# One ring of eleven buffers for loads and stores, dV and dK stored in separate halves, and dense row products on the tensor engine alone

## The chip, the cores and the metric

The kernel runs on one core of one Trainium2 chip. The metric is the device time of one execution in microseconds (us). The measured times of one kernel within one set of runs differ by up to about 1.5%, so each kernel was timed in five rounds against the kernel before on the same chip, apart from the first comparison of before and after (four runs each).

## The reference

The reference is a forward pass and its gradient: attention over a cache, a feed-forward part, the same attention again with the same weights and cache, and the same feed-forward part again. There is one query token, so every product with a weight matrix is a matrix times a vector.

```
B, Sq, D = 1, 1, 1024;  Hq, Hkv, Sk, Dh = 32, 4, 65536, 128;  F = 3584      # all bf16
x = x + attn(layernorm(x), k_cache, v_cache, wq, wo)      # called layer L1
x = x + ffn(layernorm(x), w1, b1, w2, b2)                 # L2
x = x + attn(layernorm(x), k_cache, v_cache, wq, wo)      # L3
x = x + ffn(layernorm(x), w1, b1, w2, b2)                 # L4
_out, _vjp = jax.vjp(_f, x, k_cache, v_cache, wq, wo, w1, b1, w2, b2)
return (_out, *_vjp(grad_out))                            # gradients of the caches too
```

K and V together are 128 MB. The kernel reads them four times. Sweeps 1 and 2 are the forward attentions of L1 and L3. Sweep 3 is the backward pass of L3 that finds only dq. Sweep 4 is the backward pass of L1 and makes dK and dV for both layers at once. It also stores 128 MB of dK and dV and, in the background, some 31 MB of weight gradients. Between the sweeps lie dense stages (called gap 1, gap 2, gap 3 below), which need weights but no cache.

## The kernel before

Loads of the cache come in blocks of 1 MB, 8 KB in each of 128 partitions. Six buffers of a kept pool hold blocks from one sweep to the next, which walks the other way, and six more stream. In sweep 4 the streaming six make room for staging tiles of 2 MB, two of them:

```
stpool = stack.enter_context(tc.tile_pool(name="b4_st", bufs=2))
...
def k8(g, c8):                       # eight columns of K and V at a time
    ...
    if j0 == 0:
        state["st"] = stpool.tile([P, 2, J, DH], BF, name="gst", tag="gst")   # J = 32, DH = 128
    stg = state["st"]
    ...
    for half in range(2):
        pg = ps_gg()                 # [P, 1024] f32, 2 buffers
        for t2 in range(2):          # t2 = 0 is dK, 1 is dV
            nc.tensor.matmul(pg[:, 512 * t2:512 * t2 + 512], lhsT=xt[64 * t2:64 * t2 + 64, j0 // 4 + half, :],
                             rhs=GG[64 * t2:64 * t2 + 64, :, :].rearrange("p a b -> p (a b)"), ...)
        jj = j0 + 4 * half
        evac(stg[:, :, jj:jj + 4, :]..., pg[:, :]..., kind="f32")   # ACT or DVE, whichever has less to do
    if j0 + 8 == J:                  # the block is whole: two stores of 1 MB
        nc.gpsimd.dma_start(out=GKv[g][b], in_=stg[:, 0, :, :])
        nc.gpsimd.dma_start(out=GVv[g][b], in_=stg[:, 1, :, :])
```

The softmax weights were kept as one tile for each layer, `eT[P, G, R, C]`, in which the columns c of one head are neighbours. Sweep 4 took them in two products on DVE and copied them on POOL:

```
nc.vector.tensor_tensor(out=X[:, :, 0:R],  in0=ps_dp[:, :, 0:R],  in1=ea, op=ALU.mult)
nc.vector.tensor_tensor(out=X[:, :, R:R2], in0=ps_dp[:, :, R:R2], in1=eb, op=ALU.mult)
nc.gpsimd.tensor_copy(out=X[:, :, R2:3 * R], in_=ea)
nc.gpsimd.tensor_copy(out=X[:, :, 3 * R:R4], in_=eb)
```

A dense product along the rows of a weight matrix (for which this kernel has PE transpose the weights first) was given, 128 x 1024 weights at a time, to whichever engine a running estimate called least busy: DVE multiplies and sums (A), DVE multiplies and ACT sums (B), or PE transposes and multiplies after a copy by DVE (C) or ACT (D).

```
best = min(opts, key=lambda k: (max(opts[k]), sum(opts[k])))
if best == "A":   nc.vector.scalar_tensor_tensor(..., accum_out=yout)
elif best == "B": nc.vector.tensor_tensor(...); nc.scalar.activation(..., accum_out=yout)
else:             # C, D: 8 transposes, a copy out of PSUM, 8 matmuls of one column
```

## Time and profile before

The kernel before takes 2182.95 us (median of 4 runs, 2175.93 to 2195.28). Its profiled execution has a span of 2178.0 us. I cut the span at the first matmul of each sweep with a transposed block of the cache and at the last one into its output or dq, and some 20 us lie before sweep 1. The first view is the page of the profile. Its rows of digits are 40 equal slices of the span: the clock that was granted to TensorE in tenths, the DMA engines' busy share in tenths, and what they moved.

```profile
PE 1713.9 (79%) x29802; PEld 1353.1 (62%) x29802; DVE 1238.8 (57%) x2298; ACT 1081.2 (50%) x1672; POOL 219.6 (10%) x416
...
PEclk9999998599999966999999667888888878887888
DMA  9999999889999997999999839899998999999996
GB/s 383 418 416 416 418 416 402 310 345 415 419 415 417 417 377 264 406 414 418 416 416 419 315 112 359 318 346 369 386 356 357 347 364 364 379 354 349 396 353 249
```

A row of slices at 414 to 419 GB/s is a sweep in which the transfers leave no hole: a faster engine can shorten it only at its ends. The three dips (310, 264, 112 GB/s) are the three dense stages, where the clock falls to 5 or 6 tenths. After the third, in sweep 4, no slice but one is above 390. The windows view gives the same by stretch. Its columns are the length, each engine's busy time and instruction count, the clock, the DMA share and GB/s.

```profile
395.00:432.00 37.00, 12.68 (x268) 11.42 (x267) 35.40 (x68) 5.07 (x8) 0.00 (x0) 0.50 0.77 277
800.00:850.00 50.00, 18.82 (x238) 15.71 (x238) 34.11 (x81) 26.81 (x46) 0.00 (x0) 0.53 0.78 288
1211.00:1290.00 79.00, 50.83 (x655) 43.85 (x655) 56.02 (x157) 45.69 (x69) 1.19 (x2) 0.56 0.58 210
1440.00:2060.00 620.00, 517.11 (x5982) 313.99 (x5982) 417.42 (x571) 389.38 (x417) 156.44 (x279) 0.84 0.94 366
```

In the first dense stage DVE is busy 35.4 of 37 us. In the third no engine is full: DVE, PE and ACT wait for one another. In sweep 4 (the last line) the DMA share is 0.94. The view of the staging tile says what its writers waited for, as time in us and number of waits.

```profile
its engine sat idle before it (us, times) until:
  PE ps_gg L829: 201.0, 203
  DMA out_dram<-gst: 154.4, 44
```

Waiting for PE is waiting for work. Waiting 154 us for an earlier store to land is a lack of buffers. Last, the groups of instructions that the change touches, with busy time, mean ns of one, and the idle time before them.

```profile
L143 ACT CAST gst<-ps_gg 128x1024 bf16<-128x1024 f32 x296 | 296.5, 1016 | 210.2 <-PE ps_gg L829 114.0 <-DMA out_dram<-gst 89.9 <-ACT gst L143 1.2
L146 DVE CAST gst<-ps_gg 128x1024 bf16<-128x1024 f32 x216 | 262.9, 1220 | 160.4 <-PE ps_gg L829 86.9 <-DMA out_dram<-gst 64.4 <-issue 3.1
...
L580 ACT ACTIVATE L_eT<-S_sb,L_negm 128x128 bf16<-128x128 f32 x256 | 99.1, 390 | 27.5 <-DVE L_negm L576 27.5
...
L796 DVE TENSOR_TENSOR X<-ps_sc,L_eT 128x256 bf16<-128x256 f32 x64 | 36.9, 577 | 0.0
...
L690 DVE TENSOR_TENSOR dsT<-ps_sc,L_eT 128x512 bf16<-128x512 f32 x32 | 32.6, 1019 | 31.8 <-PE ps_sc L685 31.8
```

### The profile page before, as it was taken

Reading aid. Unit: us, or ns where it says so; the run is one execution under the profiler, and the core shown is the slowest. Engines: PE = TensorE matmul, PEld = TensorE weight load, DVE = VectorE, ACT = ScalarE, POOL = GpSimd, SP = SyncE. Lnnn points to the kernel's source line nnn. Section 1 sums busy time; section 2 is a strip of 40 time slices with the busy share of each in tenths; the row PEclk is TensorE's granted clock in tenths of the full one; section 3 lists DMA queues with packets and bytes.
Section 4 is the critical chain, followed back from the end, with each engine's and each line's share of the span. In section 5 each row is a group of like instructions: output and inputs, shape, how many; then the busy total and the mean of one; then the engine's idle time right before and its main releaser. Section 6 shows DMA issues by size and latency. Waiting matters only on the chain. (4 is left out here: it accounts for less than half of the span.)

```text
span 2178.0 us, 66787 instructions
## 1 busy us (share of the span) xinstructions
PE 1713.9 (79%) x29802; PEld 1353.1 (62%) x29802; DVE 1238.8 (57%) x2298; ACT 1081.2 (50%) x1672; POOL 219.6 (10%) x416
## 2 busy tenths in 40 slices
PE   7888887488888855878787767788879888888877
PEld 6877776388777744777777655445545545445444
DVE  3545443645445437644444668666757666666766
ACT  3434443044444416543433556566656556665655
POOL 0000000000000000000000001222222222222222
PEclk9999998599999966999999667888888878887888
DMA  9999999889999997999999839899998999999996
GB/s 383 418 416 416 418 416 402 310 345 415 419 415 417 417 377 264 406 414 418 416 416 419 315 112 359 318 346 369 386 356 357 347 364 364 379 354 349 396 353 249
DMA packets 149226, 806.51 MB, mean 370 GB/s; under 512 B 14012, under 2 KB 14026, under 8 KB 69322
## 3 DMA queue, kind: packets, MB, share of 16 engines
q1 hardware_dynamic: 120714, 636.54, 74.1%
q0 software_dynamic: 28224, 165.70, 18.6%
q8 instruction: 233, 3.82, 0.7%
q14 instruction: 55, 0.45, 0.1%
HBM read 636.50 MB, written 165.69 MB: 368 GB/s over the span
## 5 line engine op out<-in xcount | busy, mean ns | idle before, releaser
L146 DVE COPY kt<-ps_tr 128x1024 bf16<-128x1024 bf16 x667 | 449.4, 686 | 366.9 <-PE ps_tr L524 191.7
L143 ACT COPY kt<-ps_tr 128x1024 bf16<-128x1024 bf16 x357 | 357.4, 1014 | 494.8 <-PE ps_tr L524 301.0
L143 ACT CAST gst<-ps_gg 128x1024 bf16<-128x1024 f32 x296 | 296.5, 1016 | 210.2 <-PE ps_gg L829 114.0
L146 DVE CAST gst<-ps_gg 128x1024 bf16<-128x1024 f32 x216 | 262.9, 1220 | 160.4 <-PE ps_gg L829 86.9
L829 PE MATMUL ps_gg<-GG,xt 64*128 64x512 bf16 x1024 | 220.9, 431 | 80.5 <-ACT gst L143 57.8
L541 PE MATMUL ps_sc<-L_qpad,kt 128*128 128x64 bf16 (+7 forms) x4096 | 196.2, 194 | 19.2 <-DVE kt L146 9.4
L769 PE MATMUL ps_tr<-ident_b,blk 128*128 128x128 bf16 x2048 | 206.7, 243 | 0.9 <-DVE ctd_rows L164 0.4
L769 PEld LDWEIGHTS <-blk 128*128 128x128 bf16 x2048 | 141.4, 108 | 79.7 <-issue 78.6
L541 PEld LDWEIGHTS <-kt 128*128 128x128 bf16 x4096 | 158.5, 100 | 38.3 <-DVE kt L146 18.3
L524 PE MATMUL ps_tr<-ident_b,blks 128*128 128x128 bf16 x2016 | 150.8, 230 | 30.1 <-DMA blks<-in_A_k_cache_dram 26.6
L524 PE MATMUL ps_tr<-ident_b,blk 128*128 128x128 bf16 x2080 | 148.6, 225 | 17.9 <-DMA blk<-in_A_k_cache_dram 17.4
L524 PEld LDWEIGHTS <-blks 128*128 128x128 bf16 x2016 | 126.5, 104 | 34.6 <-DMA blks<-in_A_k_cache_dram 30.5
L829 PEld LDWEIGHTS <-xt 64*128 64x128 bf16 x1024 | 59.7, 95 | 131.9 <-issue 101.6
L354 ACT ACTIVATE mv_t<-mv_t 128x1024 bf16<-128x1024 bf16 (+1 forms) x100 | 103.5, 1035 | 75.9 <-DVE mv_t L353 70.0
L524 PEld LDWEIGHTS <-blk 128*128 128x128 bf16 x2080 | 125.1, 101 | 21.9 <-DMA blk<-in_A_k_cache_dram 20.8
L787 PEld LDWEIGHTS <-kt 128*128 128x128 bf16 x2048 | 98.0, 106 | 51.0 <-issue 50.3
L787 PE MATMUL ps_sc<-DOB,kt 128*128 128x64 bf16 (+3 forms) x2048 | 127.5, 203 | 0.0
L870 PE MATMUL ps_gg<-rowb,rowa 2*128 2x512 bf16 x240 | 86.0, 445 | 51.9 <-ACT gst L143 22.4
L823 PE MATMUL ps_acc<-X,blk 128*128 128x64 bf16 (+1 forms) x2048 | 118.4, 202 | 0.0
L685 PE MATMUL ps_sc<-dOpad,kt 128*128 128x64 bf16 (+7 forms) x2048 | 101.1, 195 | 14.9 <-ACT kt L143 10.6
L580 ACT ACTIVATE L_eT<-S_sb,L_negm 128x128 bf16<-128x128 f32 x256 | 99.1, 390 | 27.5 <-DVE L_negm L576 27.5
L823 PEld LDWEIGHTS <-blk 128*128 128x128 bf16 x2048 | 87.9, 104 | 34.4 <-issue 33.8
(462 smaller groups left out, 2524.8 us busy)
## 6 DMA issues: line engine op xcount, KB each, us to landing
blk<-in_A_k_cache_dram SPq DMA_DIRECT2D x153, 1024.0 KB, 19.8
blk<-in_A_v_cache_dram SPq DMA_DIRECT2D x153, 1024.0 KB, 19.8
out_dram<-gst POOLq DMA_DIRECT2D x128, 1024.0 KB, 10.4
blks<-in_A_k_cache_dram SPq DMA_DIRECT2D x98, 1024.0 KB, 19.9
blks<-in_A_v_cache_dram SPq DMA_DIRECT2D x90, 1024.0 KB, 20.0
out_dram<-og POOLq DMA_DIRECT2D x116, 256.0 KB, 7.1
blks<-in_B_w_dram SPq DMA_DIRECT2D x32, 896.0 KB, 10.4
blks<-in_A_wo_dram SPq DMA_DIRECT2D x17, 1024.0 KB, 20.2
```

Of the source, the lines that this page charges most:

```text
L143: nc.scalar.copy(out=out, in_=in_)
L146: nc.vector.tensor_copy(out=out, in_=in_)
L354: nc.scalar.activation(out=t[:, 0:n], in_=t[:, 0:n], func=ACTF.Copy, accum_out=yout)
L524: nc.tensor.transpose(pt[:, i, :], kb8[:, i, :], ident_b[:, :])
L541: nc.tensor.matmul(state["ps_s"][:, s:s + w, :].rearrange("p a b -> p (a b)"), lhsT=kt[:, i, :], rhs=L["qpad"][:, g, 0:w, :].rearrange("p ...
L580: nc.scalar.activation(out=eT[:, g, h, c0:c0 + SU], in_=S[:, h, :], func=ACTF.Exp, bias=negm[:, g, su, h:h + 1], scale=SCALE, accum_out=rs ...
L685: nc.tensor.matmul(state["ps_dp"][:, s:s + w, :].rearrange("p a b -> p (a b)"), lhsT=vt[:, i, :], rhs=dOpad[:, g, 0:w, :].rearrange("p a b ...
L769: nc.tensor.transpose(pt[:, i, :], vb8[:, i, :], ident_b[:, :])
L787: nc.tensor.matmul(state["ps_dp"][:, s:s + w, :].rearrange("p a b -> p (a b)"), lhsT=vt[:, i, :], rhs=DOB[:, g, 0:w, :].rearrange("p a b - ...
L823: nc.tensor.matmul(ps_dq[:, 0:w, :].rearrange("p a b -> p (a b)"), lhsT=kb8[:, i, :], rhs=X[:, s:s + w, :].rearrange("p a b -> p (a b)"), ...
L829: nc.tensor.matmul(pg[:, 512 * t2:512 * t2 + 512], lhsT=xt[64 * t2:64 * t2 + 64, j0 // 4 + half, :], rhs=GG[64 * t2:64 * t2 + 64, :, :].re ...
L870: nc.tensor.matmul(pg[:, n0:n0 + 512], lhsT=ra[:, ka * P:(ka + 1) * P], rhs=rb[:, n0:n0 + 512], start=True, stop=True)
```

## The change

It has four parts. (1) All 1 MB buffers, for loads, kept blocks and staging, come from one ring of eleven, handed out in the order in which they come free in the program (this order is fixed when the kernel is built, so a load waits for one particular buffer); seven blocks are kept. (2) In sweep 4 the first half of a block's steps makes all of dV and the second half all of dK. Each is stored from its own 1 MB buffer when it is done, in rows of 8 KB as before. (3) The softmax weights of both layers go into one tile `E[P, G, C, 16]`, in which the 16 heads of a column are neighbours, so the product X is one instruction and the POOL copies go. (4) In the dense stages all row products go to PE, with up to seven transposed tiles made ready ahead, also before their vector is known.

```diff
-    NKEEP = 6
-    NSTREAM = 6
+    NSLOT = 11
+    NWT = 7
+    NKEEP = 7
...
+    FREE = deque(range(NSLOT))
+    class Slot:
+        def __init__(self):
+            self.i = FREE.popleft()
+            self.t = slotp.tile([P, BLK], BF, name="slot%d" % self.i, tag="slot%d" % self.i)
+        def free(self):
+            FREE.append(self.i)
...
     def ps_gg():
-        return PS["pool"].tile([P, 1024], F32, name="ps_gg", tag="gg", bufs=2)
+        return PS["pool"].tile([P, 512], F32, name="ps_gg", tag="gg", bufs=4)
...
-            if j0 == 0:
-                state["st"] = stpool.tile([P, 2, J, DH], BF, name="gst", tag="gst")
+            t = 1 if 2 * j0 < J else 0
+            j1 = (2 * j0) % J
+            if j1 == 0:
+                state["st"] = Slot()
...
-            if j0 + 8 == J:
-                nc.gpsimd.dma_start(out=GKv[g][b], in_=stg[:, 0, :, :])
-                nc.gpsimd.dma_start(out=GVv[g][b], in_=stg[:, 1, :, :])
+            if j1 + 16 == J:
+                nc.gpsimd.dma_start(out=(GVv if t else GKv)[g][b], in_=stg)
+                state.pop("st").free()
...
+    class Rows:                                   # row products on PE
+        def front(self, job, kc, slab):           # 8 transposes and a copy, no vector needed
+            ...
+        def back(self):                           # 8 matmuls of one column
+            ...
+        def run(self):
+            self.fill()                           # up to NWT tiles ahead, across jobs
+            while self.queue:
+                self.back()
+                self.fill()
...
+    rows.add(wq_rows(lastg[2]), DC, R, lambda: L3["dqT"][:, gsl(lastg[2])], fin_dx2)
+    rows.add(slabs(B_w2, 0, FC, 0, D, 4), FC, DC, lambda: dx2[:], fin_dh2)
+    rows.add(slabs(B_w1, 0, DC, 0, F, 1), DC, FC, lambda: dh2[:], fin_dx1)
+    rows.add(wo_rows(g0), R, DC, lambda: dx1[:], dO_finish(L1, g0))
+    rows.run()
```

## The prediction

> **What bounds the kernel now.** Four sweeps over a 128 MB cache, with dense stages between. The windows view shows the DMA engines at share 1.01-1.02 and 414-415 GB/s in sweeps 1, 2 and 3 (20-380, 475-795, 880-1190 us): bound by loads. Time can be saved only where DMA is not full:
>
> - first dense stage (395-432 us): share 0.77; DVE busy 35.4 of 37 us
> - second (800-850 us): 0.78
> - third (1211-1290 us): 0.58, clock 0.56
> - start of sweep 4 (1290-1440 us): 0.80
> - steady sweep 4 (1440-2060 us): 0.94, 366 GB/s, PE busy 83%
> - end (2060-2178 us): 0.81.
>
> In sweep 4 the view of the staging tile shows 44 waits, 154 us in all, of ACT and DVE for an earlier store to land; the chain of waits puts 10% of the span on those stores. Two staging tiles of 2 MB, stored when a block is whole (about 12.8 us each), leave no slack against 10.4 us median landing.
>
> **What the change does.**
>
> 1. Staging becomes 1 MB halves from the common eleven buffers, refilled about two blocks (25 us) after their release. The store waits should nearly vanish. Loads keep about six buffers, as now, but may queue behind a store.
> 2. Evacuations double in number and halve in size. From the trace: a 128x1024 one takes 1016 ns (ACT) or 1220 ns (DVE), a 128x512 one 588 or 690 ns. Two halves cost 0.16 us more than a whole: about 95 us over two engines that have room (DVE 67%, ACT 63% busy). One X product replaces two (1.02 us for 1.15); POOL copies (84 us) go.
> 3. PE's matmuls in sweep 4 stay the same in number.
> 4. The dense vector products go wholly to PE: 8 transposes (1.01 us cold, 0.61 warm) and 8 one-column matmuls (about 0.25, 0.2): 1.27 or 0.85 us a tile. The Trainium skill ("TensorE: Matmul & The Clock Gate", Part 1): the clock is halved by default, released by activity; the trace agrees: granted 0.5 at 395-432 us. First stage: 28 tiles plus the forward product, 29-42 us instead of 37: about +5. Second: 40 tiles, seven ready ahead, 5 us chain gaps covered: -6. Third: 76 tiles, 61-91 us instead of 79: -8.
> 5. Seven blocks kept instead of six: three loads fewer (7 us), but fewer buffers at a stage's start: -3.
>
> **Sum.** From 1290 us to the end 310 MB move in 888 us. At the 395-400 GB/s of windows with full DMA here, that is 780 us. I expect 40% of the gap to go, 41 us, as PE at full clock needs nearly 11 us of a block. With the dense stages (-9), kept blocks (-3): about -53 us.
>
> Predicted **2125 us**, range **2070-2170**. Chances: faster by over 2% (below 2134.8) 0.57, within 2% 0.39, slower 0.04.
>
> **What would show it.** Waits of ACT and DVE on stores below 40 us (from 154). Steady sweep 4 at share 0.97 or more and 380 GB/s or more. Sweeps 1-3 unchanged at 414 GB/s. Evacuations of 128x512 near 590/690 ns. Strided exponentials still near 390 ns. First dense stage longer, third shorter. POOL busy 80 us less.
>
> **What would make it wrong.** Loads held up behind stores in the common ring, DMA idle in sweep 4. PE staying cold in the dense stages (+20 us). Strided exponentials or doubled evacuations slowing PE in sweep 4. Or the opposite: DMA filled to 1.0, PE warm throughout: 2070 us.

## The result, and the profile after

The kernel after takes 2098.05 us (median of 4 runs, 2091.76 to 2110.86). The ratio to the kernel before is 0.9613, with a 95% interval of 0.9547 to 0.9678: 3.9% faster. A ratio here is always the mean time of one kernel's runs over the mean of the other's in the same rounds, so it is not quite the ratio of the medians quoted. The profiled execution, at 2109.1 us, was the slowest of the four. A control in five rounds (`after_again`) gave a second profile, of 2093.7 us.

Lengths in us; the last two columns are the DMA share of the stage:

| stage | before | after | control | share before | share after |
|---|---|---|---|---|---|
| sweep 1 | 352.0 | 353.5 | 352.6 | 1.01 | 1.01 |
| gap 1 | 62.9 | 66.4 | 65.6 | 0.86 | 0.81 |
| sweep 2 | 346.5 | 354.0 | 347.5 | 0.99 | 0.99 |
| gap 2 | 71.3 | 55.4 | 54.6 | 0.84 | 0.93 |
| sweep 3 | 357.7 | 357.9 | 357.2 | 1.00 | 1.01 |
| gap 3 | 84.2 | 61.4 | 61.0 | 0.55 | 0.88 |
| sweep 4 | 853.1 | 814.7 | 809.1 | 0.92 | 0.94 |
| tail | 30.3 | 25.7 | 25.7 | 0.52 | 0.41 |

So the gain is sweep 4 (38 and 44 us) and the second and third dense stages (16 and 23 us). The 7.5 us more of sweep 2 did not come again in the control (in one later profile, `no_ahead`, they did).

The page of the kernel after:

```profile
PE 1747.5 (83%) x31172; PEld 1368.0 (65%) x31172; DVE 1184.0 (56%) x2435; ACT 1121.9 (53%) x2029; POOL 139.6 (7%) x278
...
PEclk9999999579999987999999997859888888896897
DMA  9999999889999998999999996969989999999996
GB/s 381 418 416 417 417 415 403 315 323 412 408 411 418 415 369 322 375 412 416 415 419 416 384 328 233 370 233 395 390 338 422 404 394 371 420 389 375 386 411 280
```

Its windows of the same stages (the dense ones lie a little elsewhere), columns as above:

```profile
400.00:430.00 30.00, 30.00 (x570) 30.00 (x568) 9.78 (x15) 9.49 (x10) 0.00 (x0) 0.50 0.74 234
800.00:845.00 45.00, 33.92 (x784) 32.06 (x785) 17.03 (x39) 14.67 (x16) 0.00 (x0) 0.78 0.98 366
1207.00:1262.00 55.00, 52.00 (x1132) 49.74 (x1130) 33.18 (x72) 28.71 (x30) 0.00 (x0) 0.95 0.94 329
1440.00:2060.00 620.00, 547.82 (x6587) 318.88 (x6585) 461.23 (x843) 432.61 (x782) 105.77 (x197) 0.87 0.98 393
```

The third dense stage now has PE busy 52 of 55 us at a clock of 0.95, where before it had 51 of 79 us at 0.56. The first has PE busy without a hole at a clock of 0.50. Steady sweep 4 went from 0.94 and 366 GB/s to 0.98 and 393 GB/s.

All waits of ACT and DVE on stores in the kernel after, from the start of sweep 4 to the end (total us, times, longest):

```profile
ACT og L144 <- DMA out_dram<-og: 64.6, 23, 7.0
DVE og L147 <- DMA out_dram<-og: 60.1, 21, 7.8
```

No line for a staging buffer is left. These two are for the weight gradients' three small buffers (og); in the kernel before that pair stood at 15.5 and 14.1 us. The waits of ACT and DVE on all stores together thus fell from 185 us to 125 us: over half of what the staging saved came back at og. The groups of instructions:

```profile
L623 ACT ACTIVATE E<-S_sb,L_negm 128x128 bf16<-128x128 f32 x256 | 150.7, 988 | 26.5 <-DVE L_negm L619 26.5
...
L144 ACT CAST og<-ps_gg 128x512 bf16<-128x512 f32 x135 | 78.5, 593 | 79.6 <-DMA out_dram<-og 64.6 <-PE ps_gg L925 9.9 <-PE ps_acc L867 2.2
...
L843 DVE TENSOR_TENSOR X<-ps_sc,E 128x512 bf16<-128x512 f32 x64 | 43.6, 682 | 0.7 <-PE ps_sc L837 0.7
L734 DVE TENSOR_TENSOR dsT<-ps_sc,E 128x512 bf16<-128x512 f32 x32 | 22.1, 691 | 31.1 <-PE ps_sc L729 31.1
```

The exponential takes 988 ns instead of 390, now that it writes every 16th element. The two products that read the weights got cheaper: one X of 682 ns in place of two of 577, and dsT 691 ns in place of 1019.

### The profile page after: what moved, and what is told of

It is laid out like the page before. It is cut to its first block, busy times and chain, and to the rows that moved or that the text cites. A ratio compares the mean times of both kernels' runs of the same rounds, so it can differ in the third digit from the quotient of the medians.

```text
span 2109.1 us, 69960 instructions
## 1 busy us (share of the span) xinstructions
PE 1747.5 (83%) x31172; PEld 1368.0 (65%) x31172; DVE 1184.0 (56%) x2435; ACT 1121.9 (53%) x2029; POOL 139.6 (7%) x278
## 4 chain that ended last, share of the span: by engine, by line
PE 41%; DMA 34%; ACT 13%; DVE 8%; issue 3%; SPq 0%; ACTq 0%; POOL 0%; POOLq 0%; DVEq 0%
DMA out_dram<-og 9%; PE ps_gg L881 6%; PE ps_tr L566 6%; PE ps_tr L818 5%; ACT E L623 5%; PE ps_sc L584 4%; PE ps_tr L373 3%; PE ps_acc L650 3%; ACT kt L144 3%; DVE kt L147 3%; PE ps_gg L925 2%; PE ps_sc L837 2%; PE ps_acc L867 2%; PE ps_tr L849 1%; PE ps_bg L389 1%
## 5 line engine op out<-in xcount | busy, mean ns | idle before, releaser
L584 PEld LDWEIGHTS <-kt 128*128 128x128 bf16 x4096 | 158.0, 100 | 73.4 <-DVE kt L147 50.3
L623 ACT ACTIVATE E<-S_sb,L_negm 128x128 bf16<-128x128 f32 x256 | 150.7, 988 | 26.5 <-DVE L_negm L619 26.5
L623 ACT ACTIVATION_READ_ACCUMULATOR E<-S_sb,L_negm 128x1 f32 x256 | 123.3, 482 | 0.0
L144 ACT CAST og<-ps_gg 128x512 bf16<-128x512 f32 x135 | 78.5, 593 | 79.6 <-DMA out_dram<-og 64.6
L147 DVE CAST og<-ps_gg 128x512 bf16<-128x512 f32 x105 | 72.0, 689 | 78.2 <-DMA out_dram<-og 60.1
L837 PEld LDWEIGHTS <-kt 128*128 128x128 bf16 x2048 | 95.4, 104 | 30.8 <-issue 29.0
L144 ACT COPY wt<-ps_tr 128x1024 bf16<-128x1024 bf16 (+1 forms) x60 | 57.6, 966 | 105.9 <-PE ps_tr L373 103.3
L729 PE MATMUL ps_sc<-dOpad,kt 128*128 128x64 bf16 (+7 forms) x2048 | 99.1, 194 | 15.5 <-ACT kt L144 11.8
L729 PEld LDWEIGHTS <-kt 128*128 128x128 bf16 x2048 | 76.5, 99 | 32.0 <-ACT kt L144 22.3
L147 DVE COPY wt<-ps_tr 128x1024 bf16<-128x1024 bf16 (+1 forms) x92 | 59.7, 662 | 58.8 <-PE ps_tr L373 57.4
L928 POOL DMA_DIRECT2D out_dram<-og x124 | 67.3, 543 | 242.1 <-ACT og L144 104.7
L351 ACT ACTIVATE mv_t<-mv_t 128x1024 bf16<-128x1024 bf16 x56 | 59.3, 1060 | 24.6 <-DVE mv_t L350 24.5
L144 ACT COPY xt<-ps_tr 128x512 bf16<-128x512 bf16 x113 | 62.5, 596 | 11.0 <-PE ps_tr L849 10.4
```

The costliest lines, as they stand in the source:

```text
L144: nc.scalar.copy(out=out, in_=in_)
L147: nc.vector.tensor_copy(out=out, in_=in_)
L584: nc.tensor.matmul(state["ps_s"][:, s:s + w, :].rearrange("p a b -> p (a b)"), lhsT=kt[:, i, :], rhs=L["qpad"][:, g, 0:w, :].rearrange("p ...
L623: nc.scalar.activation(out=E[:, g, c0:c0 + SU, L["lr"].start + h], in_=S[:, h, :], func=ACTF.Exp, bias=negm[:, g, su, h:h + 1], scale=SCAL ...
L729: nc.tensor.matmul(state["ps_dp"][:, s:s + w, :].rearrange("p a b -> p (a b)"), lhsT=vt[:, i, :], rhs=dOpad[:, g, 0:w, :].rearrange("p a b ...
L837: nc.tensor.matmul(state["ps_dp"][:, s:s + w, :].rearrange("p a b -> p (a b)"), lhsT=vt[:, i, :], rhs=DOB[:, g, 0:w, :].rearrange("p a b - ...
```

## The experiments

Twelve kernels ran. All were correct. Medians in us; ratios are to the kernel before in the same rounds (its median was 2179.6 to 2188.1). The runs are in four groups, on three chips; across groups the ratio is the better comparison, and two ratios whose intervals overlap are not told apart here. Stage lengths are from each kernel's one profiled execution; four profiles with the same code in sweep 4 (after, control, `dense_old`, `no_ahead`) range from 809 to 815 us there, so a difference under 6 us in a stage is not read. Even this limit is too low at times: the last two kernels of the table have the same code in sweep 4 and are 17 us apart there. A difference of 10 us in a stage of one profile is a hint, no proof.

| run | median | ratio | gap 1 | gap 2 | gap 3 | sweep 4 |
|---|---|---|---|---|---|---|
| after_again | 2096.99 | 0.9605 | 65.6 | 54.6 | 61.0 | 809.1 |
| dense_old | 2141.94 | 0.9809 | 61.6 | 75.5 | 87.5 | 813.2 |
| no_ahead | 2101.18 | 0.9620 | 66.5 | 57.6 | 65.4 | 812.9 |
| before_half | 2147.91 | 0.9839 | 63.4 | 71.2 | 85.1 | 814.1 |
| old_e | 2105.49 | 0.9647 | 64.5 | 57.6 | 61.3 | 821.2 |
| whole_store | 2105.25 | 0.9636 | 66.0 | 55.5 | 63.4 | 805.8 |
| keep4 | 2083.75 | 0.9554 | 64.0 | 53.5 | 63.4 | 799.6 |
| keep6_last | 2085.25 | 0.9557 | 66.0 | 57.1 | 62.0 | 801.5 |
| split_pools | 2072.93 | 0.9496 | 56.4 | 55.6 | 62.9 | 786.6 |
| spread_og | 2073.66 | 0.9505 | 66.3 | 54.7 | 61.2 | 794.4 |
| split_keep4_spread | 2049.86 | 0.9380 | 65.5 | 51.0 | 62.6 | 768.3 |
| warm_gap1 | 2046.32 | 0.9367 | 63.1 | 55.2 | 63.0 | 751.4 |

### Control

The kernel after unchanged.

> Control: the changed kernel as it is, on the chip of this group. Ratio to before 0.961 as first measured (0.955 to 0.968). Its stages should repeat: gap after sweep 3 about 61 us (before 84), gap after sweep 2 about 55 us (before 71), sweep 4 about 815 us (before 853).

Measured: 2096.99 us, ratio 0.9605 (0.9568 to 0.9642). It is the yardstick for what follows.

### Are the dense stages worth their share by themselves?

The kernel after with the old choice among DVE, ACT and PE in the dense stages:

```diff
-    rows.add(wq_rows(lastg[2]), DC, R, ...); rows.add(slabs(B_w2, ...), ...); ... ; rows.run()
+    run(g_rowdots_mix(wq_rows(lastg[2]), DC, ..., True))     # the kernel before's rowdot, A to D
+    run(g_rowdots_mix(slabs(B_w2, 0, FC, 0, D, 4), FC, dx2[:], DC, fin_dh2, "dg2", True))
+    ...
```

> The changed kernel with the dense vector products of the kernel before (DVE, ACT and PE share them by the load model, each product after its vector is known). Theory: the dense rework is worth about 35 us (gaps 2 and 3 go back from 55 and 61 to 71 and 84 us, gap 1 from 66 to 63), so ratio to before about 0.978, with sweep 4 unchanged near 815 us. Rival: the gaps got shorter because the common ring of buffers feeds them better; then the gaps stay within 5 us of those of the changed kernel and the ratio stays near 0.963.

Measured: 2141.94 us, 45 us more than the control (35 expected). Gaps 2 and 3 are back at 75.5 and 87.5 us, a little above those of the kernel before (its scratch tiles for DVE are not quite the same), and sweep 4 is unchanged at 813.2. So the gain of the dense stages comes from their own products, not from the ring that feeds them. The windows view of gap 3 and the beginning of sweep 4, first with the old products:

```profile
1215.00:1290.00 75.00, 47.13 (x628) 39.06 (x628) 50.03 (x136) 41.53 (x61) 0.00 (x0) 0.57 0.73 256
```

and in the control:

```profile
1215.00:1290.00 75.00, 69.15 (x1227) 58.22 (x1223) 52.11 (x124) 43.97 (x63) 2.69 (x5) 0.89 0.67 238
```

The control does twice the matmuls in that time (1227 for 628), and the clock is 0.89 for 0.57.

### Is it making tiles ready ahead, or PE alone?

```diff
-            while self.jobs:
-                it, job = self.jobs.popleft()
-                for kc, slab in it:
-                    yield from self.front(job, kc, slab)
+            it, job = self.jobs.popleft()          # one job at a time; run() starts the next when it is empty
+            for kc, slab in it:
+                yield from self.front(job, kc, slab)
...
-    run(g_w1(L4, ps_mv([P, FC]), pre=rows.fill))
+    run(g_w1(L4, ps_mv([P, FC])))
```

> The changed kernel with all products still on PE, but no slab transposed before the vector of its own product is known. Theory: preparing ahead is most of the dense gain, because at each of five vector boundaries PE idles about 4 us and some of the following work runs at the halved clock: gaps 2 and 3 together 20 to 30 us longer than in the changed kernel (116 us), ratio about 0.973, granted clock in gap 3 below 0.8 instead of 0.92. Rival: what counts is that all products are on PE; then gaps 2 and 3 together are at most 10 us longer and the clock in gap 3 stays near 0.9.

Measured: 2101.18 us (ratio 0.9575 to 0.9666, so not told apart from the control); gap 2 is 3 us longer and gap 3 is 4 us longer, which is within what one profile can tell. My theory that crossing the dependence between two products is what pays fell. Giving everything to PE, which then runs at a granted clock of 0.89 in gap 3 also without preparing ahead, is what pays. One reservation: the scheduler may still lift some transposes over the vector's chain by itself.

### Is the slack of the staging enough for sweep 4?

The kernel before, with only its staging cut in two in time: four tiles for half a block in the same 32 KB, stored at each half.

```diff
-        stpool = stack.enter_context(tc.tile_pool(name="b4_st", bufs=2))
+        stpool = stack.enter_context(tc.tile_pool(name="b4_st", bufs=4))
...
+            H = J // 2
-            if j0 == 0:
-                state["st"] = stpool.tile([P, 2, J, DH], BF, name="gst", tag="gst")
+            if j0 % H == 0:
+                state["st"] = stpool.tile([P, 2, H, DH], BF, name="gst", tag="gst")
```

> The kernel before with only its staging changed: four buffers for dV and dK of half a block (8 KB per partition each, the same 32 KB in all) in place of two for a whole block, stored when a half is done. Loads keep their own pools and the dense stages are untouched. Theory A (the waits of the evictions on whole-block stores held the last sweep back): the sweep falls from 853 us to 815-830, the waits of evictions on a staging store (154 us before) fall under 50, time 2140-2155. Rival B (the common ring is what helps, since stores lend their space to loads): the sweep stays at 845-855 and the time within 10 us of 2181.

Measured: 2147.91 us, 32 us less than the kernel before; sweep 4 fell from 853.1 to 814.1 us, and the waits on staging stores from 154 to 32 us:

```profile
ACT gst L143 <- DMA out_dram<-gst: 19.1, 10, 3.1
DVE gst L146 <- DMA out_dram<-gst: 12.6, 6, 4.2
```

Theory A holds: this alone gives sweep 4 as short as the whole change does. But the two get there by different ways. I summed the time of the DMA packets inside sweep 4 over the 16 engines, per queue (load queue and store queue), and the idle rest:

| us in sweep 4 | before | before_half | control |
|---|---|---|---|
| no transfer | 68 | 30 | 50 |
| load packets | 392 | 368 | 359 |
| store packets | 388 | 412 | 396 |

With half blocks of each tensor the rows in a store are 4 KB instead of 8, and a store is 0.5 MB instead of 1. The page's DMA section shows it (packets, MB, share of the span), first before:

```profile
q0 software_dynamic: 28224, 165.70, 18.6%
```

and with half blocks:

```profile
q0 software_dynamic: 46656, 165.71, 20.0%
```

The same 159 MB in more packets go with 24 us more of store time in sweep 4. The loads lose the same 24 us, for reasons that I did not test, so that the two queues together take 780 us in both kernels. The control shows that the store time needn't have risen: its stores, with 8 KB rows, take 2.45 us per MB, those of `before_half` 2.59 and those of before 2.44. (Its load time is lower also because it loads 3 MB less there.) Whether it is the row or the size of the store was not separated. Making dV and dK one after the other keeps both: each time half as much is stored, as one store of 1 MB with rows of 8 KB. What the kernel after loses in return is new idle time, 20 us more than in `before_half`; the next experiments are about it.

### Must a slot be stored and given back early?

The kernel after, but both 1 MB stores are issued at the block's end.

```diff
-            if j1 + 16 == J:
-                nc.gpsimd.dma_start(out=(GVv if t else GKv)[g][b], in_=stg)
-                state.pop("st").free()
+            if j0 + 8 == J:
+                both = state.pop("st")
+                for tt in (1, 0):
+                    nc.gpsimd.dma_start(out=(GVv if tt else GKv)[g][b], in_=both[tt].t...)
+                    both[tt].free()
```

> The kernel after, but both 1 MB halves of a block are stored only when the block is done, and hold two slots of the ring until then; the order of the products is unchanged. Theory A (early, short holding of the slots matters): slots are held about one more half block, the sweep goes from 810 us to 825-845, time 2112-2135. Rival B (the ring's depth absorbs it: eleven slots are more than the loads need): the sweep stays within 5 us of 810, the time within 2095-2103.

Measured: 2105.25 us (between the two theories; ratio 0.9591 to 0.9682, not told apart from the control), with sweep 4 at 805.8 us. Theory A fell for the sweep, which did not grow. What grew is the tail, from 25.7 to 37.4 us: there PE waits 3.9 and 5.9 us for the two loads of wq, the weights of the last dense product, of which the second lands 28 us after its issue. In the sweep the waits moved to the load queue, where the ring's depth absorbs them. Its waits for a store to land from 1240 us on, in the control:

```profile
SPq L237 <- DMA out_dram<-slot: 154.6, 16, 20.7
...
SPq L289 <- DMA out_dram<-slot: 37.0, 5, 9.2
```

and with whole-block stores:

```profile
SPq L237 <- DMA out_dram<-slot: 495.5, 64, 24.3
...
SPq L289 <- DMA out_dram<-slot: 22.0, 5, 9.4
```

The load queue waits 518 us for stores instead of 192, and the sweep is no longer for it. Nor are the DMA engines idle for longer in it (49 us, 50 in the control): here the longer waits of the load queue did not make them run dry.

### Is one shared ring better than two pools?

```diff
+    STAGE = deque()                         # at the start of sweep 4: four of the eleven slots move here
-                state["st"] = Slot()
+                state["st"] = Slot(True)    # staging from STAGE only; loads from the other seven
-        return set([k for k in TOUCH[p + 1] if k in last][:NKEEP])
+        return set([k for k in TOUCH[p + 1] if k in last][:NKEEP - (p == 2)])
```

> The kernel after with its eleven slots parted in the last sweep: four for stores alone, seven for loads alone (and six blocks kept over in place of seven). Theory A (halves are what helps, sharing is not): the sweep stays within 6 us of 810, time 2092-2104. Rival B (sharing helps: a slot goes where it is wanted): the sweep becomes 820-840, time 2105-2130.

Measured: 2072.93 us, sweep 4 at 786.6 us. Both theories fell. I had not allowed that sharing could cost: it is 24 us faster than the control. No wait of a load for a store is left among those listed; the evacuations wait 24 us for staging stores instead:

```profile
ACT slot L144 <- DMA out_dram<-slot: 14.9, 11, 3.0
DVE slot L147 <- DMA out_dram<-slot: 9.3, 11, 1.8
```

Part of it is that one block less is kept at the start of sweep 4, which the next run takes apart. A second thing in this profile is chance and has nothing to do with the edit: gap 1, whose code is the same, took 56.4 us, 9 us less than in the control; see under the last experiment. Part of the 24 us may be it.

### How much of that is room at the start of sweep 4?

```diff
-        return set([k for k in TOUCH[p + 1] if k in last][:NKEEP])
+        return set([k for k in TOUCH[p + 1] if k in last][:NKEEP - (p == 2)])
```

> The kernel after with six blocks kept over into the last sweep instead of seven, and the shared ring as it was. Of the 24 us that the split pools gained (2073 for 2097; last sweep 787 for 809), this tells the part that one block less at the start gives. Theory A (the gain is that loads no longer wait on the landing of stores in the ring, 192 us of waits of the load queue before, none with split pools): the last sweep stays at 803-811, time 2088-2099. Rival B (the gain is room at the start of the last sweep): the last sweep falls to 785-797, time 2072-2085.

Measured: 2085.25 us, sweep 4 at 801.5 us, between the two theories. By medians the one block is 12 of the 24 us, by sweep 4 it is 8 of 22; both are at the edge of the noise. The DMA engines' idle time in the first 50 us of sweep 4 was 18 us in the control, 10 here, and 8 with split pools: with seven kept, only four buffers take new loads when the sweep begins. What remains of the gain of the split pools, 15 us of sweep 4 in one profile each, points to the parting itself; the intervals of the two ratios (0.9523 to 0.9591 here, 0.9452 to 0.9540 there) still overlap.

### Keeping fewer blocks everywhere

```diff
-    NKEEP = 7
+    NKEEP = 4
```

> The changed kernel with four blocks kept between sweeps instead of seven, so that seven buffers and not four carry the dense weights. Theory: with seven kept, DMA falls idle at the end of a sweep (share 0.34 at 790-800 us) as all buffers are full; with four kept, that hole closes and the gaps shorten, and the nine more loads (about 2.5 us each) are paid with time that DMA had idle anyway: ratio 0.955 to 0.961, gap 2 below 52 us. Rival: each block kept is a load saved, and nine more loads cost up to 22 us: ratio 0.967 to 0.971.

Measured: 2083.75 us (ratio 0.9521 to 0.9586, just overlapping the control's), 13 us faster than the control although it loads more; gap 2 is 53.5 us, where I had expected less than 52. At 760 to 800 us, where sweep 2 ends, the control's windows view shows

```profile
760.00:800.00 40.00, 26.17 (x637) 24.91 (x637) 10.63 (x35) 10.51 (x26) 0.29 (x1) 0.76 0.84 322
```

and with four kept

```profile
760.00:800.00 40.00, 24.49 (x643) 23.06 (x641) 8.96 (x32) 9.83 (x25) 0.29 (x1) 0.75 1.00 396
```

A kept block saves a load of about 2.5 us (1 MB at 415 GB/s), but it takes a buffer from the weights of the dense stage at the moment when the DMA engines have nothing else to do. Yet this hole is the smaller part: sweep 2 and gap 2 together are 3 us shorter, and sweep 4 is 9.5, about as much as in `keep6_last`, where the blocks were fewer at that turn alone. In the first 50 us of sweep 4 the DMA engines are idle for 11 us instead of 18.

### The layout of the softmax weights

The kernel after with the old layout, two X products and the POOL copies.

```diff
-                nc.scalar.activation(out=E[:, g, c0:c0 + SU, L["lr"].start + h], in_=S[:, h, :], func=ACTF.Exp,
+                nc.scalar.activation(out=L["eT"][:, g, h, c0:c0 + SU], in_=S[:, h, :], func=ACTF.Exp,
...
+                nc.gpsimd.tensor_copy(out=Ev[:, :, 0:R], in_=ea)
+                nc.gpsimd.tensor_copy(out=Ev[:, :, R:R2], in_=eb)
```

> The kernel after with the old layout of the softmax weights: exp written to neighbouring elements, the weights copied by POOL into the second product's order, and X as two products of 512 columns per half... of 256. Theory A (the layout is hidden under the transfers both ways): exp falls from 988 ns to about 390 ns, POOL rises by 80 us of busy time, and the time stays within 8 us of 2097. Rival B (the strided write costs at the ends of the first two sweeps): gap1 and gap2 shorter by 1-3 us each and the time 2085-2092. Rival C (the copies loaded the last sweep): the sweep 815-830, time 2103-2118.

Measured: 2105.49 us (ratio 0.9604 to 0.9689), sweep 4 at 821.2 us, 12 us more than the control. The exponential is back at 391 ns and POOL's busy time at 220.6 us. The numbers are those of rival C, but the intervals of the times overlap with the control's, so the layout's gain is not shown. Nor does the slow strided exponential look quite hidden under the transfers: with the old layout sweep 2 took 339.1 us, while in the eight profiles with the new one and as many blocks kept it took 346.5 to 354.0 us, with the DMA share falling to 0.34 to 0.75 in its last 10 us (0.90 here). In this pair of profiles the layout saves 11 us in sweep 4 and the tail and loses 5 us in sweep 2 and gap 2 together.

### The bursts of weight gradients

In every kernel so far the DMA share falls some 100 to 140 us into sweep 4, to between 0.54 and 0.85 in slices of 20 us. There the queue of urgent background work has just emptied, and the outer products then catch up through three og buffers (17 stores from 1350 to 1390 us in the control).

```diff
             while self.urgent:
                 if next(self.urgent[0][1], "end") == "end":
                     self.urgent.popleft()
                     continue
-                return
+                break
-            while self.normal and self.done < want:
+            one = False
+            while self.normal and self.done < want and not one:
...
                     self.done += 1
+                    one = True
```

> The kernel after, but the weight gradients' outer products are made at most one per step, also while the queue of urgent work is not empty, in place of a burst of some 15 at once when it empties. Theory A (the bursts make the holes: DMA share 0.68-0.79 at 1360-1400 us, evictions waiting 127 us on three og buffers): these waits fall under 60 us, the last sweep goes to 785-800, time 2072-2090. Rival B (the holes come from the products' clock or from urgent work itself): the last sweep stays within 6 us of 809, time 2091-2103.

Measured: 2073.66 us, sweep 4 at 794.4 us; the waits on og fell from 127 to 72 us. Theory A holds for the time and the sweep; the waits fell less than I had expected. The place of the burst in the control:

```profile
1360.00:1400.00 40.00, 35.23 (x221) 16.14 (x221) 20.90 (x39) 19.11 (x35) 8.09 (x15) 0.52 0.74 278
```

and with the products spread:

```profile
1360.00:1400.00 40.00, 38.46 (x497) 23.21 (x496) 34.87 (x76) 31.89 (x57) 7.53 (x14) 0.98 0.98 395
```

With the hole the low clock went too (0.52 to 0.98), so whether the og buffers or the cold PE made it is not separated.

### All three together

Split pools, four kept, outer products spread.

> All three together: split pools (four slots for stores, seven for loads, in the last sweep), four blocks kept over at every turn, the outer products spread. If the gains add (24 us of the split pools and 13 us of keeping four against 2097, of which some 5 are the same room at the start of the last sweep, and 10-20 us for spreading): 2040-2060. If they overlap or spreading gives nothing: 2062-2072.

Measured: 2049.86 us, ratio 0.9380 (0.9341 to 0.9419), sweep 4 at 768.3 us with a DMA share of 0.98. This is the expected first case. The three gains of 24, 13 and 23 us make 61 (unrounded); the 12 us of `keep6_last`, which split pools and four kept share, counted once, they make 49, and 47 were measured.

### The clock of the first dense stage

In gap 1 PE is busy without a hole, and in seven of the ten profiles that share its code the clock stays at 0.50 in the middle of it. The control, at 400 to 430 us:

```profile
400.00:430.00 30.00, 30.00 (x572) 30.00 (x570) 9.67 (x14) 9.38 (x10) 0.00 (x0) 0.50 0.71 241
```

The profile of `split_pools`, with the same instructions there, at the same place:

```profile
400.00:430.00 30.00, 27.42 (x712) 26.84 (x709) 13.74 (x31) 11.00 (x12) 0.00 (x0) 0.90 0.91 303
```

The first is bound by a cold PE, with a transpose taking 308 ns; the second had a transpose at 218 ns and a stage 9 us shorter. Its clock was full for 24 us of the stage; in `old_e` and `keep4` it was for 10 us. To see whether the kind of PE work decides, one useless matmul was added for each of the 28 weight tiles of the stage, to the fastest kernel:

```diff
         for _ in rows.front(dgjob, kc, slab):
             pass
+        junk = ps_sc([P, 512])
+        nc.tensor.matmul(junk[:, :], lhsT=ident_b[:, :], rhs=slab[:, 0:512], start=True, stop=True)
```

> The fastest kernel so far (split pools, four kept, outer products spread), with one useless 128x512 matmul beside each of the 28 weight tiles of the first dense stage, its result never read. There PE was busy 30.0 of 30 us and yet its clock stayed at 0.50, while in the third dense stage, with half of its matmuls transposes (a third in the first), it was 0.95. Theory A (the grant follows how much of the time the array itself works, and one-column matmuls hardly count): the clock at 400-430 us goes to 0.9-1.0, transposes from 308 to about 219 ns, and the first dense stage falls from 65.5 us to 55-61 in spite of 28 more matmuls. Rival B (the clock there is held down by something else, such as what ran before, or by chance): the clock stays near 0.5 and the stage grows to 70-78 us. The time as a whole: 2040-2048 in A, 2054-2064 in B.

Measured: 2046.32 us, ratio 0.9367 (0.9339 to 0.9395). The windows view at 400 to 425 us without the extra matmuls:

```profile
400.00:425.00 25.00, 25.00 (x477) 25.00 (x476) 7.96 (x12) 8.10 (x8) 0.00 (x0) 0.50 0.93 340
```

and with them:

```profile
400.00:425.00 25.00, 24.02 (x551) 21.13 (x550) 8.96 (x13) 9.01 (x9) 0.00 (x0) 0.98 0.92 334
```

The clock went to 0.98 and the transposes to 220 ns, as Theory A had it. This is one profile, and three of ten had some full clock without help, so chance is not excluded (the mean clocks of all its runs, 0.905 to 0.913 for 0.894 to 0.906 without, fit a release, but are means of the whole span). And the stage fell only from 65.5 to 63.1 us, where 55 to 61 were expected: each added matmul is recorded at 390 ns, 11 us for the 28, and with four blocks kept the DMA share was already 0.93 there. The time as a whole is not told apart from the kernel without them (the intervals overlap), and the sweep 4 of 751.4 us in this profile has no cause in the edit; another execution of the same code took 768.3. So the clock can be full there, and here it was worth no measurable time.

## Why the prediction was right or wrong

The predicted 2125 us was 27 us too high; the measured 2098 us lies inside the range, and "faster" was right. Point by point:

- **Sweep 4: right in mechanism, in size partly by luck.** I expected 41 us less from 1290 us to the end. Sweep 4 and the tail gave 38.4 + 4.6 = 43 us (49 in the control). The staging waits went from 154 us to none listed (the waits on all stores, though, only to 125 us, by those for og). Steady sweep 4 reached the share (0.98) and rate (393 GB/s) named beforehand. `before_half` confirms the cause. But my reason for taking only 40% of the gap, "PE at full clock needs nearly 11 us of a block", was not what set the limit. PE is busy for 708 us of sweep 4 in the control, 11 us for each of 64 blocks, and for 709 us in `split_keep4_spread`, whose sweep 4 is 41 us shorter. What was left lay in the buffers and the bursts; that 40% fitted is luck.
- **Dense stages: the mechanism was right, two terms were mis-sized.** I wrote +5, -6 and -8 us; measured were +3.5, -16 and -23. That is 35 us saved instead of 9, and nearly all of the 27 us by which the time was missed. The step that failed is "Third: 76 tiles, 61-91 us instead of 79: -8": I took a value between a cold and a warm PE. The trace shows PE busy 52 of 55 us there at a clock of 0.95 and a stage of 61.4 us, the warm end. The second stage likewise ran at 0.78. I had named "PE warm throughout" as a way to be faster. I had also put part of the gain down to tiles made ready ahead; `no_ahead` puts that at 3 to 4 us, at most, in each of the two stages.
- **The clock rule that I used.** The Trainium skill, "TensorE: Matmul & The Clock Gate", Part 1, has the clock halved by default and released after about 3.4 us of a busy PE. Gap 3 agrees (0.95). Gap 1 does not: PE was busy 30 of 30 us and stayed at 0.50, so a record of a busy engine isn't the same as what the grant goes by. With one 128x512 matmul more for each tile (`warm_gap1`) the clock was 0.98, in one profile.
- **Kept blocks: wrong sign, as far as the times tell.** I counted "-3" for seven kept blocks. `keep4` is 13 us faster than seven, and `keep6_last` 12 us. I had weighed "fewer buffers at a stage's start" and made it too small.
- **Strided exponentials: wrong.** "Strided exponentials still near 390 ns" failed: 988 ns. In sweep 1 that cost no visible time; at the end of sweep 2 it may have cost some (339.1 us in `old_e`). That the layout would cheapen dsT (1019 to 691 ns) and X (1.15 us to 0.68, where I had 1.02) I missed too. The Trainium skill, "SBUF - State Buffer", section "Door 1: The DMA port swizzle", has lines of 16 bytes, with a penalty for each access that goes to a new one. The figures agree in direction: the exponential used to write neighbouring 2-byte elements and now writes one every 32 bytes, while dsT used to read its weights 1 KB apart and now reads eight together.
- **Evacuations and POOL: right.** 593 and 689 ns for 128x512 (588 and 690 said); POOL 80.0 us less (80 said).
- **"Loads held up behind stores in the common ring": named as a risk, and it was real.** The control's load queue waits 192 us for stores. `whole_store` shows that such waits need not cost, but parting the ring (`split_pools` against `keep6_last`) still gave 12 us by medians, at the edge of the noise.

Adding up: the staging in halves is worth 32 us (`before_half` against before), the dense products 45 us (`dense_old` against the control), the layout about 8 us (`old_e` against the control, within the noise). That makes 85 us, and the control is 84 us below before. By this sum the ring and the seventh kept block, the largest part of the diff, brought nothing net. That is not shown: the first part is measured by adding it to before, the other two by taking one from after, and by the intervals of the ratios each is uncertain by 10 to 12 us. That the ring and the kept blocks cost something is better founded: split pools with six kept gave 24 us. With four kept and spread outer products, a matter of the background work and not of the ring, it came to 47: 2049.86 us against 2096.99.

Still open: why the same instructions in gap 1 ran partly at full clock in three profiles without help; whether the strided exponential costs time in sweep 2; and which part of the split pools' remaining gain comes from loads not waiting and which from a more even flow of stores.

## What to carry to other kernels

Look at where the transfers have holes and ask of each hole what buffer or engine was wanted: here two staging tiles, three small buffers fed in bursts, and blocks kept for later each made one. A sum of waits does not say what they cost. 154 us of waits of the evacuations held sweep 4 back, and 518 us of the load queue's in `whole_store` did not; yet `split_pools`, which traded 192 us of the load queue's for 24 us of the evacuations', was faster. So ask of each wait whether the DMA engines run dry behind it. And in a stage that several engines share while PE is cold, try giving PE whole products: here gaps 2 and 3 became 16 and 23 us shorter in spite of the extra transposes, as the clock rose, while gap 1, where it stayed at 0.50, became 3 us longer.

## What the Trainium skill lacked or had wrong

- "TensorE: Matmul & The Clock Gate", Part 1: that a busy short window releases the clock is not enough. With PE recorded busy 30.0 of 30.0 us on transposes and one-column matmuls, the clock stayed at 0.50; with one 128x512 matmul added for each tile it was 0.98, and in one profile of ten the same code had 0.90 without.
- The same page, Part 4, says of one kernel that the full clock doesn't engage for transposes, since they don't count as a busy PE in the same way. That would fit gap 1, but not gap 3: there half of PE's matmuls were transposes, nearly all the rest had one column, the clock was 0.95 and a transpose took 219 ns, against 308 ns at 0.50.
- "ScalarE: Activation LUTs", section "What ACT_TABLE_LOAD costs", gives about 280 ns + 0.833 ns an element for an activation with a pointer bias. For 128 elements an estimate from it is 387 ns, and 390 ns were measured as long as the output was contiguous. Written 32 bytes apart the same activation took 988 ns, and the read of its accumulator 482 ns instead of 188. The page has nothing on the stride of the output; "SBUF - State Buffer" ("Door 1") has a rule that would explain it, without a figure; no run here tests it.
- "DMA: Bandwidth & Descriptors", section "Where 436 GB/s comes from", says without a condition that between HBM and SBUF about 358 GB/s binds, while a note just above it has that only for both cores of a pair streaming. Here, on one core, loads alone ran at 414 to 419 GB/s in most slices of sweeps 1 to 3, as the note has it.
- The same page's rule of large transfers says nothing of rows of 4 or 8 KB in stores that run beside loads on this chip: 159 MB of stores in sweep 4 took 388 us of packet time with rows of 8 KB and 412 us when the rows were 4 KB (and the stores 0.5 MB instead of 1).
